# Second attention's scores on half arrays, two experts side by side

## The chip, the cores and the metric

The kernel runs on one core of a Trainium2 chip. The metric is the device time of one execution in microseconds; "before" is the median of three executions. A profile of one execution shows each engine's instructions in time: TensorE (PE for its matmuls, PEld for its weight loads), VectorE (DVE), ScalarE (ACT), GpSimd (POOL) and the DMA queue that SyncE (SP) issues to.

## The reference

The kernel computes three layers in a row: a windowed attention, a gated MLP, and a mixture of four attention experts. Only the last is touched by the change:

```python
def _moe2_ref(x, w_gate, wq, wk, wv, wo):          # x: 4 x 576 x 512, 4 experts, Hd = 64
    logits = x @ w_gate
    ...
    for e in range(E):
        q = x @ wq[e]; k = x @ wk[e]; v = x @ wv[e]
        scores = scale * (q @ k.transpose(0, 2, 1))
        scores = np.where(causal, -1000000000.0, scores)
        scores = scores - scores.max(-1, keepdims=True)
        a = np.exp(scores)
        a /= a.sum(-1, keepdims=True) + 1e-09
        ye = a @ v @ wo[e]
        ...                                         # weighted by the two best experts of a token
```

## The kernel before, in words

Precision comes from splitting: a float32 value is kept as a high part in the format float32r and a low part, the rounded difference. A product of two split values is three matmuls (high x high, high x low, low x high) accumulated in one PSUM bank.

**Order of the work.** Every piece of work is a node of a planner (class `Planner`, function `N`) with its engine or engines, a cost, the tiles it takes and the tiles it uses. The program is made of two plans that run one after the other (first attention and MLP, then the experts). In each, the planner walks through time and gives each engine the ready node of the lowest priority number; the table `SHIFT` moves units of work, `SWITCH` is added for a matmul node of another `form` (another division of TensorE's array) than the last, and `DRAIN` is what the planner books for such a change. The result is a fixed order on each engine.

**Banks.** PSUM has eight banks of 128 x 512 float32; they form one ring, `bank`, from which projections, scores, transposes and P V products all take.

**The experts.** Four batches (`b`), two pairs of experts (`pr`), two experts in a pair (`e` or `x`). The pair's q and k have 128 rows: expert 0 in rows 0 to 63, expert 1 in rows 64 to 127 (`HALF`).

- `c_qk` projects q or k of a pair for one half of the 576 tokens (288 columns, 12 matmuls) and splits the result. Each expert gets its own tiles: `qs[x]` holds the high part of q in the expert's own half and its low part in the other half; `kd[x]` holds the high part of k twice, in both halves (`twin` copies it over); `kz` (rings `r_kl`) holds the low part of k in the own half and zeros in the other (`zeros` fills them once). All these copies and subtractions work on 64 rows at a time.
- `unit` does one tile of 128 query rows of one expert: scores, mask and maximum, exponential with its sum, reciprocal, scaling of P by the sum and by the expert's weight, transpose of P, copy of it to `pg`. Query tile `I` = 0 to 3 sees 128 x (I + 1) keys. The scores (`s_mm`) are two matmuls over all 128 rows: (high, low) q against (high, high) k in `kd`, and the same q against (low, zero) k in `kz`, which together are the three products. The fifth tile (`last`) holds the last 64 queries of both experts, in two column halves of 288; there each half is four matmuls, two of them with 64 columns of weights, into one bank.
- `c_pv` multiplies P by v, two experts in the two column halves of the array; `c_wo` applies the output projection and stores.

Of the kernel before, what the change touches and what calls it, by code (L numbers as in the profile page):

```python
# [26 lines left out]
SWITCH = 107920.0  # L27
A_BIAS = 10098.0
C_BIAS = 162315.0
DVE_BIAS = (1136.0, 1147.0)  # L30
POOL_BIAS = (1131.0, 1068.0)
# [3 lines left out]
EFT = (636.0, 778.0)  # L35
# [54 lines left out]
class Node:  # L90
    __slots__ = ("on", "emit", "prio", "wait", "next", "ready", "alloc", "use", "end", "by", "late", "form", "nth", "sbuf")


class Planner:

    LAT = 200.0, 165.0, 130.0, 75.0, 900.0
    ISSUE, WAY, RATE, FLIGHT = 475.0, 650.0, 360.0, 8  # L100

    DRAIN = (0.0, 145.0, 145.0), (0.0, -78.0, 0.0), (0.0, 0.0, -78.0)

    CLASH, BEHIND = 1.0, 2200.0
# [164 lines left out]
def attn_gmlp_moe_kernel(ctx: ExitStack, tc: tile.TileContext, kq0, qT, kT, v, w_in, wspT, b_sp, w_outT,  # L269
# [30 lines left out]
    r_y = [Ring(lambda i=i: keep.tile([128, 2, S], F32, tag=f"y{i}", name=f"y{i}", bufs=1), 1, True) for i in range(6)]  # L300
# [875 lines left out]
    def unit(b, pr, e, I):  # L1176
# [3 lines left out]
        if last and e:  # L1180
            return
# [246 lines left out]
```

## Time and profile before

| | |
|---|---|
| time, median of 3 runs | 448.05 us (447.97, 448.05, 448.39) |
| span of the profiled execution | 447.1 us, mean granted clock of TensorE 1.000 |
| the profiled execution's own time | not recorded apart from the three runs; 448.05 - 447.1 = 0.95 us is taken for what lies around the span |
| TensorE busy | 438.9 us, 98% of the span, 3962 matmuls |
| TensorE weight loads busy | 396.0 us, 89% |
| VectorE, ScalarE, GpSimd busy | 310.9, 293.1, 107.4 us |

Busy times of TensorE contain overlaps: a matmul's row lasts from its start to its last result, and the next one starts before that. What one costs is read from one start to the next. The profile's groups name tiles, `bank<-kd,qs` being a matmul that writes `bank` and reads `kd` and `qs`; 128*64 is the part of the array it uses, rows by columns.

### The profile page before, as it was taken

What the parts mean: (1) busy time and instruction counts of PE and PEld (TensorE: products, weight loads), DVE (VectorE), ACT (ScalarE), POOL (GpSimd) and SP (SyncE); (2) the same over time, 40 slices, a digit from 0 to 9 for tenths busy, and PEclk for the clock granted to TensorE, in tenths of its full rate; (3) what the DMA queues carried; (4) which work ended last, traced back from release to release, by engine and by line L of the source; (5) the groups of instructions that cost most, each with busy time, mean ns of one, the idle gap of its engine ahead of it and who ended that gap; (6) DMA issues with size and microseconds to landing.
All of it is one profiled execution on the core that took longest, in us unless ns stands there. A gap on an engine that the chain in (4) does not pass through costs nothing.

```text
span 447.1 us, 10829 instructions
## 1 busy us (share of the span) xinstructions
PE 438.9 (98%) x3962; PEld 396.0 (89%) x3962; DVE 310.9 (70%) x1241; ACT 293.1 (66%) x926; POOL 107.4 (24%) x154
## 2 busy tenths in 40 slices
PE   8999999999999999999999999999999999999996
PEld 7977899989899879998899999789899978897875
DVE  4989989962875988024544556998697987787650
ACT  4989989662676969203322346987675978777863
POOL 4335782400310126000200251610031011011110
PEclk9999999999999999999999999999999999999999
DMA  7994837140242605003001000000010001000114
GB/s 280 281 330 122 251 101 221 45 140 0 64 138 64 179 7 144 0 1 95 1 1 48 0 1 1 1 2 1 1 48 25 1 2 48 0 2 25 71 53 160
DMA packets 31079, 33.10 MB, mean 74 GB/s; under 512 B 1905, under 2 KB 24689, under 8 KB 31026
## 3 DMA queue, kind: packets, MB, share of 16 engines
q1 hardware_dynamic: 31026, 32.41, 23.4%
q8 instruction: 31, 0.51, 0.5%
q14 instruction: 22, 0.18, 0.1%
HBM read 27.68 MB, written 4.72 MB: 72 GB/s over the span
## 4 chain that ended last, share of the span: by engine, by line
PE 87%; DVE 6%; ACT 4%; issue 2%; POOL 1%; POOLq 0%; ACTq 0%; DVEq 0%
PE bank L333 79%; PE bank L1238 5%; PE bank L564 3%; DVE p L1207 1%; ACT pa L552 1%; DVE qs L357 1%; POOL p L1222 1%; DVE p L1222 1%; ACT p L1218 1%; DVE pa L546 0%; ACT pa L558 0%; DVE pa L560 0%; DVE kz L357 0%; ACT pg L344 0%; ACT kd L344 0%
## 5 line engine op out<-in xcount | busy, mean ns | idle before, releaser
L333 PE MATMUL bank<-xh,w 128*128 128x288 f32 x512 | 109.6, 298 | 0.0
L333 PEld LDWEIGHTS bank<-xh,w 128*128 128x128 f32 x512 | 84.1, 188 | 0.9 <-DVE st L767 0.2
L333 PE MATMUL bank<-xl,w 128*128 128x288 f32 x256 | 75.3, 294 | 0.0
L333 PE MATMUL bank<-w,xh 128*128 128x512 f32 (+1 forms) x256 | 64.7, 342 | 0.2 <-ACT pt L344 0.2
L552 ACT ACTIVATE pa<-pa,mx 128x128 f32<-128x128 f32 x144 | 55.9, 400 | 5.4 <-DVE mx L546 5.4
L333 PEld LDWEIGHTS bank<-xl,w 128*128 128x128 f32 x256 | 48.2, 188 | 0.4
L333 PEld LDWEIGHTS bank<-w,xh 128*128 128x128 f32 x256 | 43.2, 188 | 5.7 <-ACT pt L344 0.5
L1218 ACT ACTIVATE p<-p,mc 128x128 f32<-128x128 f32 (+4 forms) x72 | 41.8, 582 | 8.4 <-DVE mc L1207 7.7
L1222 POOL TENSOR_SCALAR p<-p,mc,fx 128x256 f32<-128x256 f32 (+4 forms) x26 | 17.1, 658 | 111.3 <-DVE mc L1221 52.2
L333 PE MATMUL bank<-w,xl 128*128 128x512 f32 (+1 forms) x128 | 43.2, 338 | 0.0
L333 PE MATMUL bank<-wsp_h,vh 128*128 128x288 f32 x128 | 38.6, 302 | 0.0
L333 PE MATMUL bank<-wsp_h,vl 128*128 128x288 f32 x128 | 37.7, 295 | 0.0
L333 PE MATMUL bank<-wsp_l,vh 128*128 128x288 f32 x128 | 37.7, 294 | 0.0
L1207 DVE CUSTOM_DVE_ANT_0 p<-bank,cmask 128x128 f32<-128x128 f32 (+4 forms) x72 | 33.2, 482 | 5.2 <-PE bank L333 4.2
L770 POOL TENSOR_TENSOR st<-st,nhalf 128x1 f32<-128x1 f32 (+1 forms) x20 | 12.3, 615 | 98.7 <-DVE st L769 98.7
L344 ACT ACTIVATE pg<-bank 128x128 f32<-128x128 f32 (+4 forms) x71 | 29.1, 440 | 5.2 <-PE bank L1238 4.7
L546 DVE CUSTOM_DVE_ANT_0 pa<-bank,mask 128x128 f32<-128x128 f32 x120 | 28.4, 284 | 5.9 <-POOL mx L415 4.1
L1238 PE MATMUL bank<-ident,p 128*128 128x128 f32 x192 | 30.1, 278 | 1.5 <-POOL p L1222 0.7
L333 PE MATMUL bank<-kd,qs 128*128 128x128 f32 (+5 forms) x96 | 30.5, 335 | 0.0
L552 ACT ACTIVATION_READ_ACCUMULATOR pa<-pa,mx 128x1 f32 x144 | 28.6, 199 | 0.0
L333 PE MATMUL bank<-kz,qs 128*128 128x128 f32 (+5 forms) x96 | 28.4, 313 | 0.0
L835 DVE TENSOR_TENSOR y<-bank,ut 128x288 f32<-128x288 f32 x24 | 10.9, 454 | 24.9 <-PE bank L333 24.9
(209 smaller groups left out, 1083.4 us busy)
## 6 DMA issues: line engine op xcount, KB each, us to landing
vt<-in_v_dram SPq DMA_DIRECT2D x12, 512.0 KB, 4.9
qa<-in_qT_dram SPq DMA_DIRECT2D x44, 96.0 KB, 3.8
out_dram<-ot SPq DMA_DIRECT2D x15, 256.0 KB, 2.0
y<-in_w_in_dram SPq DMA_DIRECT2D x7, 512.0 KB, 7.3
kt<-in_kT_dram SPq DMA_DIRECT2D x12, 288.0 KB, 5.0
y<-in_w_outT_dram SPq DMA_DIRECT2D x4, 512.0 KB, 4.5
y<-in_wspT_dram SPq DMA_DIRECT2D x2, 576.0 KB, 4.2
vt<-in_kq_dram SPq DMA_DIRECT2D x2, 384.0 KB, 4.4
```

The costliest lines, as they stand in the source:

```text
L333: pe.matmul(o, lhsT, rhs, start=start, stop=stop)
L344: act.activation(o, i, AF.Copy)
L357: engs[e].tensor_tensor(out=o, in0=a, in1=hi.bitcast(F32), op=ALU.subtract)
L546: dve.tensor_tensor_reduce(out=pa[:, j, :], in0=ps[:, j * 128:(j + 1) * 128], in1=mask(j), scale=-0.125, scalar=3.0e38, op0=ALU.add, op1=A ...
L552: act.activation(pa[:, j, :], pa[:, j, :], AF.Exp, bias=mx[:, j, 0:1], scale=-1.0, accum_out=mx[:, j, 1:2])
L564: pe.transpose(ps2[:, j * 128:(j + 1) * 128], pa[:, j, :], ident)
L770: a = N((POOL, 464), lambda e: pool.tensor_tensor(out=st[:m, 9:10], in0=st[:m, 8:9], in1=nhalf[:m], op=ALU.pow), [n1], use=[st])
L835: dve.tensor_tensor(out=o, in0=ps[:, :HS], in1=u[:, d, tk], op=ALU.mult)
L1207: dve.tensor_tensor_reduce(out=P[:, a0:a1], in0=ps[:, :w], in1=msk, scale=-0.125, scalar=3.0e38, op0=ALU.add, op1=ALU.min, accum_out=mc[:, ...
L1218: a = N((ACT, 284 + 0.87 * L), lambda e: act.activation(P[:m, :L], P[:m, :L], AF.Exp, bias=mc[:m, 0:1], scale=-1.0, accum_out=mc[:m, 2:3]) ...
L1222: a = N({POOL: 328 + 0.832 * L, DVE: 90 + 0.52 * L}, lambda e: engs[e].tensor_scalar(P[:, :L], P[:, :L], mc[:, 3:4], fx[:, I, ev:ev + 1], ...
L1238: pe.transpose(ps[:, j * m:(j + 1) * m], P[:, j * 128:(j + 1) * 128], ident)
```

## The change

q and k of a pair are kept as plain parts in one tile `qk` of 128 rows and 4 x 576 columns: q high, q low, k high, k low, each with expert 0 in the upper and expert 1 in the lower rows. A score is then three products over 64 rows, and the same product of the two experts is issued one behind the other, on the upper and on the lower half of the array's rows, into two banks. Tiles 0 and 1 share one node and the same two banks; the fifth tile takes two nodes, each with two banks. Masking of the fifth tile is done in two pieces of 64 rows. The twin copies and the zero fills of `kz` go. P tiles become a ring of five that are freed in any order (before: four, in order). A fourth `form` is told to the planner, and the constants of its order (`SWITCH`, `DVE_BIAS`, `POOL_BIAS`, `EFT`, and the later entries of `SHIFT`) are other ones.

```diff
-    DRAIN = (0.0, 145.0, 145.0), (0.0, -78.0, 0.0), (0.0, 0.0, -78.0)
+    DRAIN = (0.0, 145.0, 145.0, 145.0), (0.0, -78.0, 0.0, 0.0), (0.0, 0.0, -78.0, 0.0), (0.0, 0.0, 0.0, 0.0)
...
-SWITCH = 107920.0
+SWITCH = 137658.0
...
+    r_qk = ring(p2, "qk", [128, 4 * S], F32R, 3)
...
-    r_p = ring(p2, "p", [128, S], F32, 4)
+    r_p = Ring(None, 5, tiles=[p2.tile([128, S], F32, name=f"p{i}") for i in range(5)])
...
     def c_qk(b, pr, h, nm):
...
-            def hi(e):
-                for x in range(2):
-                    copy(e, kd[x][HALF[x], tk], ps[HALF[x], :HS])
...
-            def twin(e):
-                for x in range(2):
-                    copy(e, kd[x][HALF[1 - x], tk], kd[x][HALF[x], tk])
...
+        a = N(on_copy(HS), lambda e: copy(e, qk[:, hi], ps[:, :HS]), [a], use=[ps, qk])
+        a = N((DVE, t_tt(HS)), lambda e: sub(e, qk[:, lo], ps[:, :HS], qk[:, hi]), [a], use=[ps, qk])
...
+    def scores(b, pr, tiles, prio):
+        qk = QK[b, pr]
+        def three(outs, q, k0, k1):
+            for n, (x, y) in enumerate(((0, 0), (0, 1), (1, 0))):
+                for e in range(2):
+                    mm(outs[e], qk[HALF[e], x * S + q[e]:x * S + q[e] + 128],
+                       qk[HALF[e], (2 + y) * S + k0:(2 + y) * S + k1], n == 0, n == 2)
...
+        ps, pp = [r_sc.new(), r_sc.new()], [r_p.new(), r_p.new()]
...
+        a = N((PE, sum(3 * t_mm(128 * I + 128) for I in tiles)), go, deps, alloc=ps + pp, use=[qk], prio=prio, form=3)
...
     def unit(b, pr, e, I):
...
+        if (b, pr, I) not in SC:
+            scores(b, pr, [0, 1] if I < 2 else [I], prio)
...
-                for x, c0, c1 in [(1, 448, S), (0, 512, S)] if last else [(e, 128 * I, 128 * I + m)]:
-                    mm_all(ps[:c1 - c0, :a1 - a0], [(qs[x][:, c0:c1], k[x][:, a0:a1]) for k in (kd, kl)])
...
+                    for y in range(2):
+                        dve.tensor_tensor_reduce(out=P[HALF[y], a0:a1], in0=ps[y][HALF[y], :HS],
...
```

On TensorE, the first scores of the second half, batch 0, pair 0. Before:

```order
L333 MATMUL bank_69<-kd,qs 128x128
L333 MATMUL bank_69<-kz_3559,qs 128x128
L333 MATMUL bank_66<-kd,qs 128x256
L333 MATMUL bank_66<-kz_3559,qs 128x256
L333 MATMUL bank_71<-kd,qs 128x128
L333 MATMUL bank_71<-kz_3560,qs 128x128
L333 MATMUL bank_72<-kd,qs 128x256
L333 MATMUL bank_72<-kz_3560,qs 128x256
```

The same scores (tiles 0 and 1 of both experts) with the change:

```order
L333 MATMUL bank_68<-qk 128x128
L333 MATMUL bank_69<-qk 128x128
L333 MATMUL bank_68<-qk 128x128
L333 MATMUL bank_69<-qk 128x128
L333 MATMUL bank_68<-qk 128x128
L333 MATMUL bank_69<-qk 128x128
L333 MATMUL bank_68<-qk 128x256
L333 MATMUL bank_69<-qk 128x256
L333 MATMUL bank_68<-qk 128x256
L333 MATMUL bank_69<-qk 128x256
L333 MATMUL bank_68<-qk 128x256
L333 MATMUL bank_69<-qk 128x256
```

Eight matmuls into four banks, expert by expert, have become twelve into two banks, the experts alternating.

On TensorE, a little later, around the first P V product (64x256 and 64x128 on `pg`), before:

```order
L333 MATMUL bank_72<-kd,qs 128x288
L333 MATMUL bank_72<-kz_3560,qs 128x288
L333 MATMUL bank_72<-kd,qs 64x288
L333 MATMUL bank_72<-kz_3559,qs 64x288
L333 MATMUL bank_68<-pg_3882,v_3583 64x256 x2
L333 MATMUL bank_68<-pg_3882,v_3583 64x128 x2
L333 MATMUL bank_70<-w,xh 128x260 x2
```

and with the change:

```order
L333 MATMUL bank_66<-qk 128x384
L333 MATMUL bank_71<-qk 128x384
L333 MATMUL bank_69<-pg_3855,v_3629 64x256 x2
L333 MATMUL bank_69<-pg_3855,v_3629 64x128 x2
L333 MATMUL bank_72<-qk 128x288
L333 MATMUL bank_68<-qk 128x288
L333 MATMUL bank_72<-qk 128x288
L333 MATMUL bank_68<-qk 128x288
L333 MATMUL bank_72<-qk 128x288
L333 MATMUL bank_68<-qk 128x288
L333 MATMUL bank_73<-xh,w 128x288
```

The P V product stands between two groups of scores now. Over the whole order, scores stood in 42 groups and P V products in 13 before; now scores stand in 21 and P V products in 9, and 12 times one of them follows the other directly.

On ScalarE, the copies of the first projections, before:

```order
L344 ACTIVATE kd<-bank_73 64x288 x2
L344 ACTIVATE kd<-kd 64x288 x2
L344 ACTIVATE v_3583<-bank_70 128x256
L344 ACTIVATE v_3583<-bank_68 128x256
L344 ACTIVATE v_3583<-bank_69 128x256
L344 ACTIVATE kd<-bank_66 64x288 x2
L344 ACTIVATE kd<-kd 64x288 x2
```

and with the change:

```order
L344 ACTIVATE qk<-bank_73 128x288
L344 ACTIVATE v_3629<-bank_70 128x256
L344 ACTIVATE qk<-bank_68 128x288
L344 ACTIVATE v_3629<-bank_69 128x256
L344 ACTIVATE qk<-bank_66 128x288
L344 ACTIVATE v_3629<-bank_71 128x256
L344 ACTIVATE v_3629<-bank_72 128x256
```

Four 64-row copies for each half of k, two of them twins, have become one copy of 128 rows.

## Rows read from the trace of the kernel before

**Rows 1.** Cores: span, mean granted clock of TensorE.
```profile
core 0: 447.1 us, clock 1.000
```

**Rows 2.** Stretches of time: busy us of PE, PEld, DVE, ACT, POOL (instructions), clock, DMA.
```profile
280.00:300.00 20.00, 19.23 (x143) 16.65 (x143) 19.34 (x84) 17.59 (x54) 9.48 (x10) 1.00 0.01 2
...
400.00:420.00 20.00, 20.00 (x143) 16.91 (x142) 15.80 (x67) 16.24 (x45) 3.60 (x6) 1.00 0.07 27
```

**Rows 3.** Waits of PE, 260 to 448 us: total us, times, longest us.
```profile
PE bank L1238 <- POOL p L1222: 0.7, 3, 0.3
PE bank L1238 <- DVE mc L1220: 0.5, 1, 0.5
PE bank L1238 <- DVE p L1222: 0.2, 1, 0.2
```

**Rows 4.** Instructions on tile kd: its matmuls, ns min/median/max.
```profile
L333 PE MATMUL bank<-kd,qs x96: 220/331/487, 279.5 to 424.8; 128*128 128x128 f32 x16, 128*128 128x256 f32 x16, 128*128 128x384 f32 x16, 128*128 128x512 f32 x16
```

**Rows 5.** PE in order of time, three stretches with scores: start us, latency us.
```profile
339.73 0.34 PE L333 MATMUL bank<-kd,qs 128*128 128x384 f32 x1
...
340.07 0.40 PE L333 MATMUL bank<-kd,qs 128*128 128x512 f32 x1
...
340.53 0.22 PE L333 MATMUL bank<-kd,qs 128*128 128x128 f32 x1
...
415.88 0.28 PE L333 MATMUL bank<-kd,qs 128*128 128x256 f32 x1
...
416.36 0.30 PE L333 MATMUL bank<-kd,qs 128*128 128x288 f32 x1
...
417.42 0.63 PE L333 MATMUL bank<-w,oh 128*128 128x512 f32 x2
...
424.64 0.23 PE L333 MATMUL bank<-kd,qs 128*128 128x128 f32 x1
...
425.04 1.59 PE L333 MATMUL bank<-w,ot 128*128 128x512 f32 x6
```

**Rows 6.** PE in order of time, first attention: three transposes and what follows.
```profile
20.18 0.49 PE L564 MATMUL bank<-ident,pa 128*128 128x128 f32 x3
20.51 0.39 PE L333 MATMUL bank<-ident 128*128 128x128 f32 x2
```

**Rows 7.** PE in order of time around a score step of the first attention.
```profile
82.22 0.82 PE L564 MATMUL bank<-ident,pa 128*128 128x128 f32 x6
82.97 0.89 PE L333 MATMUL bank<-kt,qa 64*64 64x128 f32 x24
83.78 0.40 PE L333 MATMUL bank<-xh,w 128*128 128x288 f32 x1
...
84.15 0.43 PE L333 MATMUL bank<-xh,w 128*128 128x288 f32 x2
```

**Rows 8.** Groups of weight loads by form: busy us, mean ns.
```profile
L333 PEld LDWEIGHTS bank<-kd,qs 128*128 128x128 f32 x80 | 15.3, 192 | 0.7 <-ACT v L344 0.2 <-issue 0.2
...
L333 PEld LDWEIGHTS bank<-kt,qa 64*64 64x64 f32 x432 | 11.6, 132 | 2.1 <-issue 0.8 <-DVE mx L546 0.3 <-DVE mx L570 0.2
```

**Rows 9.** Groups of DVE and ACT from 262 us on, half-height pieces: mean ns.
```profile
L357 DVE TENSOR_TENSOR qs<-bank,qs 64x288 fp32r<-64x288 f32 x32 | 14.6, 455 | 4.5 <-ACT qs L344 2.9 <-PE bank L1238 1.0
...
L344 ACT ACTIVATE kd<-kd 64x288 fp32r<-64x288 f32 x32 | 14.1, 440 | 0.5
...
L344 ACT ACTIVATE qs<-bank 64x288 fp32r<-64x288 f32 x32 | 12.9, 404 | 6.6 <-PE bank L333 6.2
```

**Rows 10.** Instructions on y and ut: full-height pieces of 288 columns, ns min/median/max.
```profile
L835 DVE TENSOR_TENSOR y<-bank,ut x24: 429/457/458, 73.4 to 199.3; 128x288 f32<-128x288 f32 x24
...
L352 ACT ACTIVATE ut<-bank x29: 384/410/414, 56.1 to 229.4; 128x288 f32<-128x288 f32 x29
```

More of the change, by code (lines that the diff above doesn't have):

```diff
@@ L26 @@
 N_Q = 6
-SWITCH = 107920.0
+SWITCH = 137658.0
 A_BIAS = 10098.0
 C_BIAS = 162315.0
-DVE_BIAS = (1136.0, 1147.0)
-POOL_BIAS = (1131.0, 1068.0)
+DVE_BIAS = (1104.0, 1251.0)
+POOL_BIAS = (1122.0, 1447.0)
 WARM = 8
@@ L34 @@
 LOADS = (-130000, -120000, -43801, -5807, 14591, 18276, 34028)
-EFT = (636.0, 778.0)
+EFT = (622.0, 777.0)
 U_CUT = 6
@@ L286, in attn_gmlp_moe_kernel @@
     ctx.enter_context(tc.manual_schedule())
-    ordered = ("xh", "xl", "xt", "kt", "vt", "pt", "vr", "vh", "vl", "qs", "kd", "v2", "vt2", "zt0", "zt1", "pg0", "pg1", "oh", "ol", "ot0", "ot1")
+    ordered = ("xh", "xl", "xt", "kt", "vt", "pt", "vr", "vh", "vl", "qk", "v2", "vt2", "zt0", "zt1", "pg0", "pg1", "oh", "ol", "ot0", "ot1")
     def ring(pl, tag, shape, dt, bufs):
@@ L969, in attn_gmlp_moe_kernel @@
     p2 = ctx.enter_context(tc.tile_pool(name="p2", bufs=1, reuse_waits="tile"))
-    r_kd = ring(p2, "kd", [128, S], F32R, 4)
-    KZ = [p2.tile([128, S], F32R, name=f"kz{i}") for i in range(4)]
+    r_qk = ring(p2, "qk", [128, 4 * S], F32R, 3)
     PG1 = [p2.tile([128, 4, 2, 320], F32, name=f"pg1{i}") for i in range(2)]
@@ L982, in zeros @@
     def zeros(pr):
-        for e in range(2):
-            i = 2 * pr + e
-            zero(("k", pr, e), [KZ[i][HALF[1 - e]].bitcast(F32)], 590.0)
         zero(("p", pr), [PG1[pr][HALF[1 - x], 3, :, x * 64:(x + 1) * 64] for x in range(2)], 200.0)
-    r_qs = ring(p2, "qs", [128, S], F32R, 4)
-    r_kl = [fixed(KZ[x::2]) for x in range(2)]
     r_v2 = ring(p2, "v2", [128, 4, 256], F32, 2)
@@ L1017, in y_deps @@
         return [n for c in range(NP) for n in ZN[b, c]], [s for c in range(NP) for s in YS[b, c]]
-    QS, KD, KL, QK_N, QK_PE = {}, {}, {}, {}, {}
+    QK, QK_N, QK_PE = {}, {}, {}
     def c_qk(b, pr, h, nm):
@@ L1025, in c_qk @@
         zn, zs = y_deps(b)
-        first = QK_PE.setdefault((b, pr, nm), [])
+        first = QK_PE.setdefault((b, pr), [])
         new = []
-        if h == 0 and nm == "q":
-            QS[b, pr] = new = [r_qs.new(), r_qs.new()]
-        elif h == 0:
-            KD[b, pr] = [r_kd.new(), r_kd.new()]
-            KL[b, pr] = [r.new() for r in r_kl]
-            new = KD[b, pr] + KL[b, pr]
+        if not first:
+            QK[b, pr] = r_qk.new()
+            new = [QK[b, pr]]
+        qk = QK[b, pr]
+        c = ("q", "k").index(nm) * 2 * S + h * HS
+        hi, lo = slice(c, c + HS), slice(c + S, c + S + HS)
         a = N((PE, 12 * t_mm(HS)), lambda e: mm3(ps[:, :HS], [
@@ L1036, in c_qk @@
               zn + W2_N[nm] + first, alloc=[ps] + new, use=zs + [wh, wl])
-        QK_PE[b, pr, nm] = [a]
-        if nm == "q":
-            qs = QS[b, pr]
-            def hi(e):
-                for x in range(2):
-                    copy(e, qs[x][HALF[x], tk], ps[HALF[x], :HS])
-            def lo(e):
-                for x in range(2):
-                    sub(e, qs[x][HALF[1 - x], tk], ps[HALF[x], :HS], qs[x][HALF[x], tk])
-            a = N(halves(HS), hi, [a], use=[ps] + qs)
-            a = N((DVE, 2 * t_tt(HS) + 185), lo, [a], use=[ps] + qs)
-        else:
-            kd, kl = KD[b, pr], KL[b, pr]
-            def hi(e):
-                for x in range(2):
-                    copy(e, kd[x][HALF[x], tk], ps[HALF[x], :HS])
-            def lo(e):
-                for x in range(2):
-                    sub(e, kl[x][HALF[x], tk], ps[HALF[x], :HS], kd[x][HALF[x], tk])
-            def twin(e):
-                for x in range(2):
-                    copy(e, kd[x][HALF[1 - x], tk], kd[x][HALF[x], tk])
-            n1 = N(halves(HS), hi, [a], use=[ps] + kl + kd)
-            n2 = N((DVE, 2 * t_tt(HS) + 185), lo, [n1], use=[ps] + kl + kd)
-            n3 = N(halves(HS, False), twin, [n1], use=kd, sbuf=True)
-            a = N({DVE: 0.0}, lambda e: None, [n2, n3])
+        QK_PE[b, pr] = first or [a]
+        a = N(on_copy(HS), lambda e: copy(e, qk[:, hi], ps[:, :HS]), [a], use=[ps, qk])
+        a = N((DVE, t_tt(HS)), lambda e: sub(e, qk[:, lo], ps[:, :HS], qk[:, hi]), [a], use=[ps, qk])
         QK_N.setdefault((b, pr, nm), []).append(a)
@@ L1174, in attn_gmlp_moe_kernel, with go @@
     PG, PG_N, OT, O_N, OT2, O2_N = {}, {}, {}, {}, {}, {}
+    SC = {}
+    def scores(b, pr, tiles, prio):
+        qk = QK[b, pr]
+        def three(outs, q, k0, k1):
[3 more added lines that the diff above has]
+                       qk[HALF[e], (2 + y) * S + k0:(2 + y) * S + k1], n == 0, n == 2)
+        deps = QK_N[b, pr, "q"] + QK_N[b, pr, "k"]
+        if tiles == [4]:
+            P, mc = r_p.new(), r_mc.new()
+            SC[b, pr, 4] = [], [], [P], mc
+            for i in range(2):
+                ps = [r_sc.new(), r_sc.new()]
+                a = N((PE, 3 * t_mm(HS)), lambda _, ps=ps, i=i: three(
+                    [p[:, :HS] for p in ps], (S - 64, S - 128), i * HS, (i + 1) * HS),
+                      deps + SC[b, pr, 4][0], alloc=ps + ([] if i else [P, mc]), use=[qk], prio=prio, form=3)
+                SC[b, pr, 4][0].append(a)
+                SC[b, pr, 4][1].append(ps)
+            return
+        ps, pp = [r_sc.new(), r_sc.new()], [r_p.new(), r_p.new()]
+        def go(_):
+            c = 0
+            for I in tiles:
+                w = 128 * I + 128
+                three([p[:, c:c + w] for p in ps], (w - 128, w - 128), 0, w)
+                c += w
+        a = N((PE, sum(3 * t_mm(128 * I + 128) for I in tiles)), go, deps, alloc=ps + pp, use=[qk], prio=prio, form=3)
+        c = 0
+        for I in tiles:
+            SC[b, pr, I] = a, ps, pp, c
+            c += 128 * I + 128
     def unit(b, pr, e, I):
@@ L1184, in unit @@
         ev = 2 * pr + e
-        both = range(2) if last else [e]
-        qs, kd, kl = QS[b, pr], KD[b, pr], KL[b, pr]
-        parts = [(0, HS), (HS, S)] if last else [(0, L)]
-        P, mc = r_p.new(), r_mc.new()
         fx, _, fn = FX[b]
-        tops = []
-        for i, (a0, a1) in enumerate(parts):
-            ps = r_sc.new()
-            def s_mm(_, ps=ps, a0=a0, a1=a1):
-                for x, c0, c1 in [(1, 448, S), (0, 512, S)] if last else [(e, 128 * I, 128 * I + m)]:
-                    mm_all(ps[:c1 - c0, :a1 - a0], [(qs[x][:, c0:c1], k[x][:, a0:a1]) for k in (kd, kl)])
-            def s_top(_, ps=ps, a0=a0, a1=a1, i=i):
-                w = a1 - a0
-                if not last:
-                    msk = cmask[:, 512 - L:512]
-                else:
-                    msk = cmask[:, 0:w] if i == 0 else tmask
-                dve.tensor_tensor_reduce(out=P[:, a0:a1], in0=ps[:, :w], in1=msk, scale=-0.125, scalar=3.0e38,
-                                         op0=ALU.add, op1=ALU.min, accum_out=mc[:, i:i + 1])
-            zn = [n for x in both for n in Z_N["k", pr, x]]
-            a = N((PE, 50 + 2 * len(both) * t_mm(a1 - a0, m)), s_mm, QK_N[b, pr, "q"] + QK_N[b, pr, "k"] + zn, alloc=[ps],
-                  use=[x[y] for x in (qs, kd, kl) for y in both], prio=prio)
-            tops.append(N((DVE, t_tt(a1 - a0)), s_top, [a] + tops[:1], alloc=[P, mc] if i == 0 else [],
-                          use=[ps] + ([] if i == 0 else [P, mc]), prio=prio))
@@ L1215, in unit @@
-        if len(parts) == 2:
-            tops = [N((DVE, 70), lambda e: dve.tensor_reduce(out=mc[:m, 0:1], in_=mc[:m, 0:2], axis=AX.X, op=ALU.min), tops, use=[mc], prio=prio)]
-        a = N((ACT, 284 + 0.87 * L), lambda e: act.activation(P[:m, :L], P[:m, :L], AF.Exp, bias=mc[:m, 0:1], scale=-1.0,
-                                                              accum_out=mc[:m, 2:3]), tops, use=[P, mc], prio=prio)
-        a = N((DVE, 70), lambda e: dve.tensor_scalar(mc[:m, 3:4], mc[:m, 2:3], 1e-9, None, op0=ALU.add), [a], use=[mc], prio=prio)
@@ L1221, in unit, with s_top @@
-        a = N((DVE, 75), lambda e: dve.reciprocal(mc[:m, 3:4], mc[:m, 3:4]), [a], use=[mc], prio=prio)
+        sn, banks_, pp, c0 = SC[b, pr, I]
+        P, mc, c0 = (pp[0], c0, 0) if last else (pp[e], r_mc.new(), c0)
+        cs = slice(c0, c0 + L)
+        if last:
+            tops = []
+            for i, (n, ps) in enumerate(zip(sn, banks_)):
+                a0, a1 = i * HS, (i + 1) * HS
+                def s_top(_, ps=ps, a0=a0, a1=a1, i=i):
+                    for y in range(2):
+                        dve.tensor_tensor_reduce(out=P[HALF[y], a0:a1], in0=ps[y][HALF[y], :HS],
+                                                 in1=cmask[HALF[y], 0:HS] if i == 0 else tmask[HALF[y]], scale=-0.125,
+                                                 scalar=3.0e38, op0=ALU.add, op1=ALU.min, accum_out=mc[HALF[y], i:i + 1])
+                tops.append(N((DVE, 2 * t_tt(HS) + 60), s_top, [n] + tops, use=ps + [P, mc], prio=prio))
+        else:
+            ps = banks_[e]
+            tops = [N((DVE, t_tt(L)), lambda _, ps=ps: dve.tensor_tensor_reduce(
+                out=P[:, cs], in0=ps[:, cs], in1=cmask[:, 512 - L:512], scale=-0.125, scalar=3.0e38,
+                op0=ALU.add, op1=ALU.min, accum_out=mc[:, 0:1]), [sn], alloc=[mc], use=[ps, P], prio=prio)]
@@ new lines, in unit @@
+        if last:
+            tops = [N((DVE, 70), lambda e: dve.tensor_reduce(out=mc[:, 0:1], in_=mc[:, 0:2], axis=AX.X, op=ALU.min), tops, use=[mc], prio=prio)]
+        a = N((ACT, 284 + 0.87 * L), lambda e: act.activation(P[:, cs], P[:, cs], AF.Exp, bias=mc[:, 0:1], scale=-1.0,
+                                                              accum_out=mc[:, 2:3]), tops, use=[P, mc], prio=prio)
+        a = N((DVE, 70), lambda e: dve.tensor_scalar(mc[:, 3:4], mc[:, 2:3], 1e-9, None, op0=ALU.add), [a], use=[mc], prio=prio)
@@ L1222, in unit @@
+        a = N((DVE, 75), lambda e: dve.reciprocal(mc[:, 3:4], mc[:, 3:4]), [a], use=[mc], prio=prio)
         a = N({POOL: 328 + 0.832 * L, DVE: 90 + 0.52 * L}, lambda e: engs[e].tensor_scalar(
-            P[:, :L], P[:, :L], mc[:, 3:4], fx[:, I, ev:ev + 1], op0=ALU.mult, op1=ALU.mult), [a, fn],
+            P[:, cs], P[:, cs], mc[:, 3:4], fx[:, I, ev:ev + 1], op0=ALU.mult, op1=ALU.mult), [a, fn],
               use=[P, mc, fx], prio=prio, sbuf=True)
@@ L1237, in tr @@
             for j in range(nj):
-                pe.transpose(ps[:, j * m:(j + 1) * m], P[:, j * 128:(j + 1) * 128], ident)
+                pe.transpose(ps[:, j * m:(j + 1) * m], P[:, c0 + j * 128:c0 + (j + 1) * 128], ident)
         def tc_(e_):
```

6 rows, old and new, of the table SHIFT are left out of this document.

## Prediction

> **What bounds the kernel now.** I read the span and clock first, then busy time by stretches, then what TensorE waited for, then the scores' own instructions and their order in time. The profiled execution spans 447.1 us at full granted clock [rows 1]; the median of the three runs is 448.05 us, so 0.95 us lie around the span, and I carry that over unchanged. The clock stays where it is: the change takes no long pause into TensorE's stream.
>
> In the two stretches shown from the second attention TensorE is busy 19.23 and 20.00 of 20 us, VectorE 19.34 and 15.80, ScalarE 17.59 and 16.24 [rows 2]. A busy TensorE includes overlapping ends, so the second reading is what it waited for: from 260 us on only 1.4 us in all (0.7, 0.5 and 0.2), each time a transpose waiting for a normalised P [rows 3]. So the second half runs at TensorE's pace, and what TensorE issues is what the time is made of. VectorE is the next one behind it, close in the first stretch only.
>
> **Durations.** The length of one matmul row is its latency. What it costs is the distance from its start to the next start. In [rows 5]: four 256-column score matmuls start within 0.48 us, 0.12 each; eight 288-column ones within 1.06, 0.1325 each, whether their weights have 128 columns or 64; two of 384 columns within 0.34, 0.17 each; two of 512 within 0.46, 0.23 each; four of 128 within 0.40, 0.10 each. Short ones cannot go below what their weights cost: three 128-column transposes take 0.33 us, 0.11 each [rows 6].
>
> **What is removed on TensorE.** The 96 matmuls on kd [rows 4] have as many on kz: 192. For one batch and one pair of experts: two experts, two matmuls each, for 128, 256, 384 and 512 keys, 4 x (0.10 + 0.12 + 0.17 + 0.23) = 2.48 us; the last tile, eight of 288 columns, 1.06. Together 3.54, times 8 (4 batches, 2 pairs) = 28.3 us.
>
> **What is added on TensorE.** 288 half-array matmuls, which are 144 rounds of two: three rounds for each width, six of 288 columns. If the two halves run side by side, a round costs what one full matmul of that width costs, with 0.11 as floor: 3 x (0.11 + 0.12 + 0.17 + 0.23) + 6 x 0.1325 = 1.89 + 0.80 = 2.69; times 8 = 21.5 us. That is 6.8 us less.
>
> No row of before has two halves with 128 columns of weights each. The nearest are the first attention's scores on quarter arrays: 24 instructions of 64 rows by 64 columns start and end within 0.81 us [rows 7]. One after the other at 0.11 they would need 2.64, so they run four at a time, upper and lower rows among them. But these are fp32 and move 128 columns in 0.11, half the rate of the 256 columns in 0.12 that the halves must keep up. So the bounds for the rounds are 21.5 us (side by side) and 43.0 us (one after the other); I take 21.5, by the row that is nearest. The Trainium skill (TensorE: Matmul & The Clock Gate, section Measured speedup vs the span model) reports 3.07 times, not 4, for four row tiles of 512 columns. By that the rounds would cost 28.0 us, my estimate from that page, and the sum below would turn from a gain of 2.1 us into a loss of 4.4; no row of before shows which.
>
> **Changing the array's division.** This is the cost that the change adds. A visit of the first attention's scores shows it: from the first of six transposes at 82.22 to the second-next projection matmul at 84.15 are 1.93 us [rows 7]; the work in it is 6 x 0.11 + 6 rounds x 0.11 + 2 x 0.1325 = 1.59. The other 0.34 us went into one change to quarters and one back: 0.17 each. Before, only the 64-column P V products leave the full array in the second half, 13 visits with 26 changes. By the new order there are 21 visits of scores and 9 of P V, 12 times directly next to each other: 48 changes. 22 more at 0.17 = 3.7 us. On top, the first load of each score visit has nothing to hide behind, and it is 128 columns wide where the quarters load 64: 192 against 132 ns [rows 8], 0.06 x 21 = 1.3 us. Bounds: a change could cost as little as 0.09 (the part that shows ahead of the quarters: six transposes need 0.66, and the quarters start 0.75 after them) with the first load hidden, 2.0 us in all; or, if one change of halves also empties what the other half holds, 0.25 and the load, 6.8.
>
> **Other engines.** q and k are split in one full-height piece. A half-height subtraction takes 455 ns [rows 9] and a full-height one of the same width 457 [rows 10]: height is free. So VectorE loses 64 x 0.455 and gains 32 x 0.457, less 14.5 us; the last tile's masked pass is cut into halves, 16 more at the 0.455 of such a piece, plus 7.3: net 7 us less. ScalarE loses about 64 copies of 0.404 and 32 twins of 0.440 [rows 9] and gains 32 of 0.410 [rows 10]: 27 us less. None of it lies on the path, since TensorE hardly waits; the most it can return is the 1.4 us of waits [rows 3]. The four zero fills go from POOL, off the path. What could take something back: a score step now asks for two of the eight banks and two of the five P tiles at once, so six softmax chains start together where before they started one by one. Bounds for the waits: all 1.4 us gone, or 2 us more (four waits like the longest, 0.5); I take 0.3 less, since the chains get shorter on both engines. DMAs, output stores and the first attention keep their order but for a handful of operations that change engine.
>
> **Sum.** -6.8 + 3.7 + 1.3 - 0.3 = -2.1 us against the profiled span, and so against the median: **445.9 us**.
>
> **Rivals.**
> 1. *A change of division is cheap for halves.* They divide rows only, and the columns stay whole, so perhaps only the emptying ahead of a visit is paid: 22 x 0.10 and no first load. Against it: the visit of the quarters lost as much again on the way in and out [rows 7]. -6.8 + 2.0 - 0.3 = -5.1, 442.9 us. Chance 0.13.
> 2. *The gain goes into waits.* In the first batch little other work is there to cover the six chains that start together, and near the end of the last batch as well; there VectorE is at 19.34 of 20 us already [rows 2]. The waits on P [rows 3] grow by 2 us instead of falling: -6.8 + 3.7 + 1.3 + 2.0 = +0.2, 448.2 us. For it: bursts of scores that fill all eight banks. Against it: 7 us less on VectorE, 27 less on ScalarE. Chance 0.14.
> 3. *The halves hinder each other (slower).* If the weight loads of upper and lower rows go one after the other, a round takes at least 2 x 0.11 = 0.22: 3 x (3 x 0.22 + 0.23) + 6 x 0.22 = 3.99, times 8 = 31.9 us, 10.4 more than side by side; -2.1 + 10.4 = +8.3, 456 us. One after the other altogether would be +19. It decides from the point where a round costs a tenth more than one full matmul (2.1 of 21.5). Against it: the quarters' four loads and matmuls fit one round of 0.11. For it: nothing here runs two halves at the full rate. The skill's rule above is a milder form, 452 us. Chance 0.15, both forms together.
> 4. *Changes cost 0.25 and nothing else gives*: -6.8 + 6.8 = 0, 448 us. Chance 0.06.
>
> **How the numbers follow.** About 0.9 us (0.2%) is what a measurement can tell from no change. The forecast has 0.52 and a range of its own of 444.2 to 447.4; a tenth of it falls within 0.9 us of before. Faster: 0.47 + 0.13 + a little of the second rival = 0.63. Same: 0.05 + most of rivals 2 and 4 = 0.17. Slower: 0.15 and the bad ends of 2 and 4 = 0.20. The range that should hold 8 in 10 goes from the first rival's 442.9 up over rivals 2 and 4, with another 1.2 us of waits: 442.9 to 449.4; most of rival 3 stays outside.
>
> **What would show it.** Side by side: in the order in time the two matmuls of a round start within some 10 ns and rounds of 288 columns follow at 0.13, of 512 at 0.23; rival 3 shows 0.22 or more for 288. The changes: 0.17 lost ahead of and behind each visit, with a first round longer by the load. The waits of TensorE after 260 us stay near 1.4 us; several us there are rival 2. The half copies and twins are gone from ScalarE. I am wrong if the rounds are not at one matmul's pace, or if the stream of TensorE is shorter by 2 us and the time is not.

## The result and the profile after

The changed kernel takes 442.62 us (median of 4 runs, 442.44 to 444.11); the kernel before took 448.18 us beside it (4 runs, 447.97 to 448.39). The ratio is 0.9887, with a 95% interval of 0.9871 to 0.9903: 5.6 us faster. The forecast was 445.9 us, 2.1 us faster, with a range from 442.9: right in direction, but the gain came out more than twice as large and just outside the range.

The core's span and clock, for [rows 1]:

```profile
core 0: 440.5 us, clock 0.999
```

The same two stretches of the second half as in [rows 2] (busy us of PE, PEld, DVE, ACT, POOL, then clock and DMA):

```profile
280.00:300.00 20.00, 20.00 (x182) 18.37 (x182) 14.68 (x62) 14.04 (x41) 6.08 (x7) 1.00 0.00 1
400.00:420.00 20.00, 19.86 (x144) 15.09 (x145) 16.89 (x75) 15.47 (x43) 2.15 (x3) 1.00 0.14 53
```

In the first stretch TensorE is now busy throughout. It issues 182 matmuls instead of 143, but 58 of them are half-array scores, where 35 full-array ones stood before. Meanwhile VectorE falls from 19.34 to 14.68 us and ScalarE from 17.59 to 14.04. The view of the waits, which showed 1.4 us for TensorE before [rows 3], shows none from 255 us on.

The instructions on the new tile `qk` (ns min/median/max, first and last start), for [rows 4, 9, 10]:

```profile
L333 PE MATMUL bank<-qk x288: 217/294/499, 276.8 to 414.5; 64*128 64x288 f32 x48, 64*128 64x128 f32 x24, 64*128 64x256 f32 x24, 64*128 64x384 f32 x24
L344 ACT ACTIVATE qk<-bank x32: 390/410/414, 263.2 to 399.5; 128x288 fp32r<-128x288 f32 x32
L357 DVE TENSOR_TENSOR qk<-bank,qk x32: 437/458/460, 265.8 to 400.0; 128x288 fp32r<-128x288 f32 x32
```

A full-height copy takes 410 ns and a full-height subtraction 458, as the prediction took from half-height 404 and 455. So half of each is gone, and the 32 twins with them.

TensorE in order of time around the first visit of scores (start us, latency us):

```profile
276.42 0.30 PE L333 MATMUL bank<-xl,w 128*128 128x288 f32 x1
276.55 0.29 PE L333 MATMUL bank<-xh,w 128*128 128x288 f32 x1
276.77 1.48 PE L333 MATMUL bank<-qk 64*128 64x128 f32 x18
278.19 0.40 PE L333 MATMUL bank<-xh,w 128*128 128x288 f32 x1
278.43 0.29 PE L333 MATMUL bank<-xl,w 128*128 128x288 f32 x1
```

The row `x18` merges eighteen half-array matmuls (three rounds each of 128, 256 and 384 columns); they take 1.42 us from 276.77 to 278.19. From the trace's single starts, the two of a round begin 0 to 15 ns apart, mostly 3 or 4. Inside a visit a round takes, as the median, 0.112 us (128 columns), 0.120 (256), 0.133 (288), 0.174 (384) and 0.233 (512): a full matmul's pace in [rows 5]. The first round of each visit takes longer, by 0.05 us at 128 columns and 0.10 at the wider ones.

The share of the chain of work that ended last, by engine, from the page of the changed kernel:

```profile
PE 95%; DVE 4%; issue 0%; ACT 0%; POOL 0%; POOLq 0%; ACTq 0%; DVEq 0%
```

and from the page of the kernel before, run once more (the first experiment):

```profile
PE 88%; DVE 6%; ACT 2%; issue 1%; POOL 1%; POOLq 0%; ACTq 0%; DVEq 0%
```

Before, about an eighth of that chain ran over other engines. The prediction did not read this view.

**An account of the second half.** From the first projection of the experts to the start of the last matmul, before takes 181.95 us (181.99 in the repeat) and the changed kernel 176.61: 5.3 us less, nearly the whole gain. To split it, I went through TensorE's starts in the trace: wherever the next one came more than 0.11 us later than its width's pace allows, the excess over the pace counts as lost (P V products, whose starts are uneven, only when far off). This gives 3.1 us in before (3.2 in the repeat) and 0.4 after. The view of the waits shows 1.4 us in before. So by this count the gain is 2.7 us of lost time and 2.6 us of the stream itself. The split depends on the limit: at 0.25 us instead of 0.11, lost time is 2.5 us before and 0.3 after, 2.2 less, and the stream 3.2 less. Below, "lost" is the sum with 0.11.

### The profile page after: what moved, and what is told of

It is laid out like the page before. It is cut to its first block, busy times and chain, and to the rows that moved or that the text cites. A ratio compares the mean times of both kernels' runs of the same rounds, so it can differ in the third digit from the quotient of the medians.

```text
span 440.5 us, 10970 instructions
## 1 busy us (share of the span) xinstructions
PE 434.4 (99%) x4058; PEld 390.5 (89%) x4058; DVE 291.2 (66%) x1225; ACT 268.5 (61%) x871; POOL 105.7 (24%) x157
## 4 chain that ended last, share of the span: by engine, by line
PE 95%; DVE 4%; issue 0%; ACT 0%; POOL 0%; POOLq 0%; ACTq 0%; DVEq 0%
PE bank L333 86%; PE bank L1235 5%; PE bank L564 4%; DVE p L1202 1%; DVE p L1209 1%; DVE pa L546 1%; DVE p L1219 0%; DVE pa L560 0%; PE bank L1252 0%; DVE mc L1218 0%; DVE ot L348 0%; DVE bank L686 0%; DVE y L696 0%; DVE y L688 0%; ACT ot L344 0%
## 5 line engine op out<-in xcount | busy, mean ns | idle before, releaser
L1215 ACT ACTIVATE p<-p,mc 128x384 f32<-128x384 f32 (+4 forms) x72 | 41.5, 578 | 16.9 <-DVE mc L1209 14.7
L1219 POOL TENSOR_SCALAR p<-p,mc,fx 128x128 f32<-128x128 f32 (+4 forms) x33 | 20.4, 620 | 110.8 <-DVE mc L1218 64.5
L1209 DVE CUSTOM_DVE_ANT_0 p<-bank,cmask 128x384 f32<-128x384 f32 (+3 forms) x64 | 28.6, 486 | 8.6 <-PE bank L333 8.2
L344 ACT ACTIVATE pg<-bank 128x512 f32<-128x512 f32 (+4 forms) x79 | 30.1, 438 | 2.3 <-PE bank L1235 2.0
L552 ACT ACTIVATION_READ_ACCUMULATOR pa<-pa,mx 128x1 f32 x144 | 29.8, 207 | 0.0
L1235 PE MATMUL bank<-ident,p 128*128 128x128 f32 x192 | 27.4, 276 | 0.1
L333 PE MATMUL bank<-qk 64*128 64x288 f32 (+4 forms) x288 | 27.2, 325 | 0.0
L333 PEld LDWEIGHTS bank<-w,xl 128*128 128x128 f32 x128 | 24.1, 188 | 2.8
```

Of the source, the lines that this page charges most:

```text
L333: pe.matmul(o, lhsT, rhs, start=start, stop=stop)
L344: act.activation(o, i, AF.Copy)
L552: act.activation(pa[:, j, :], pa[:, j, :], AF.Exp, bias=mx[:, j, 0:1], scale=-1.0, accum_out=mx[:, j, 1:2])
L1209: tops = [N((DVE, t_tt(L)), lambda _, ps=ps: dve.tensor_tensor_reduce(out=P[:, cs], in0=ps[:, cs], in1=cmask[:, 512 - L:512], scale=-0.125 ...
L1215: a = N((ACT, 284 + 0.87 * L), lambda e: act.activation(P[:, cs], P[:, cs], AF.Exp, bias=mc[:, 0:1], scale=-1.0, accum_out=mc[:, 2:3]), to ...
L1219: a = N({POOL: 328 + 0.832 * L, DVE: 90 + 0.52 * L}, lambda e: engs[e].tensor_scalar(P[:, cs], P[:, cs], mc[:, 3:4], fx[:, I, ev:ev + 1], ...
```

## The experiments

**The kernel before once more.** No edit. The two first profiles already differ by 1.3 us where the second half starts (261.25 and 259.98 us), ahead of nearly everything the change touches.

> The kernel before, unchanged, profiled once more. In the two profiles the first half (up to the first projection of the experts) took 261.25 us before and 259.98 after, with the same TensorE order. Theory 'chance': the 1.3 us are a matter of the execution, and this profile starts its second half anywhere from 259.9 to 261.3, most likely near 260.0. Theory 'constants': it starts at 261.2 again. The second half should take 182.0 us to the last matmul in both.

447.79 us, span 446.0; its second half starts at 260.08 us and takes 181.99. The 1.3 us in the first half is chance; the 5.3 in the second is not. TensorE's longest wait in this run, in order of time:

```profile
288.23 0.22 PE L333 MATMUL bank<-kd,qs 128*128 128x128 f32 x1
288.29 0.27 PE L333 MATMUL bank<-kz,qs 128*128 128x128 f32 x1
289.09 0.55 PE L1238 MATMUL bank<-ident,p 128*128 128x128 f32 x3 [0.53 <-DVE mc L1220]
```

The bracket says 0.53 us of idle time; from start to start it is 0.80 where a matmul of 128 columns costs 0.11, so 0.69 is lost. The view counts idle time from a matmul's modelled end, which lies 0.27 us behind its start, and so misses what overlaps with that latency. What the transposes waited for, from the chain of waits of this run (start us, us, what):

```profile
286.77 0.37 DVE p L1207
287.14 0.01 DVE mc L1207
287.15 0.07 DVE mc L1220
287.21 0.33 DVE ol L357
287.55 0.07 DVE mc L1221
287.62 0.05 DVE mc L1216
287.67 1.36 DVE p L1222
289.03 0.07 DVE mc L1220
289.10 0.53 PE bank L1238 x3
```

The chain runs on VectorE: maxima, reciprocals, a split and the scaling of P follow one another without a gap.

**Relief alone.** The kernel before with its full-array scores and its order, but q and k copied and split in one piece of 128 rows, and no twins:

```diff
-                for x in range(2):
-                    copy(e, qs[x][HALF[x], tk], ps[HALF[x], :HS])
+                copy(e, qs[0][:, tk], ps[:, :HS])
...
-                for x in range(2):
-                    sub(e, kl[x][HALF[x], tk], ps[HALF[x], :HS], kd[x][HALF[x], tk])
+                sub(e, kl[0][:, tk], ps[:, :HS], kd[0][:, tk])
...
-                for x in range(2):
-                    copy(e, kd[x][HALF[1 - x], tk], kd[x][HALF[x], tk])
+                pass
```

> The kernel before, its scores on the full array, in its own order on every engine, but q and k split in one piece of 128 rows each and without twin copies: the experts' own layout is left out, so both experts' scores are computed from the same tiles and the output is another one. ScalarE does about 27 us less and VectorE 15 us less; TensorE's matmuls are as before. Theory 'relief pays by itself': TensorE's 3.6 us of waits in the second half (182.0 us) fall to about 0.5 and the time to about 445.3 us. Theory 'relief pays only with the new order' (the new order was made for short splits, the old one for long ones): less than 1 us, 447.3 or more.

445.56 us, ratio 0.9951 (0.9938 to 0.9965): 2.2 us gained with not one matmul removed. The two experts' own layout is left out here, so the output is another one; the number and the shapes of TensorE's matmuls are those of before. Its stretches:

```profile
280.00:300.00 20.00, 19.88 (x157) 17.49 (x158) 17.73 (x83) 14.70 (x46) 9.29 (x10) 1.00 0.00 1
400.00:420.00 20.00, 20.00 (x143) 16.69 (x142) 13.36 (x57) 13.54 (x37) 3.18 (x5) 1.00 0.13 49
```

TensorE is busy 19.88 us of the first stretch, against 19.23 before [rows 2], and issues 157 matmuls in it instead of 143. Lost time falls from 3.1 to 1.4 us. The prediction had put this very part off the path and allowed 0.3 us for it.

**The changed kernel without the one-piece split.** Copies and subtractions of q and k in two 64-row pieces; scores, order and the missing twins stay:

```diff
-        a = N(on_copy(HS), lambda e: copy(e, qk[:, hi], ps[:, :HS]), [a], use=[ps, qk])
-        a = N((DVE, t_tt(HS)), lambda e: sub(e, qk[:, lo], ps[:, :HS], qk[:, hi]), [a], use=[ps, qk])
+        a = N(on_copy(HS), lambda e: [copy(e, qk[HALF[x], hi], ps[HALF[x], :HS]) for x in range(2)], [a], use=[ps, qk])
+        a = N((DVE, t_tt(HS)), lambda e: [sub(e, qk[HALF[x], lo], ps[HALF[x], :HS], qk[HALF[x], hi]) for x in range(2)], [a], use=[ps, qk])
```

> The changed kernel with the copies and subtractions of q and k issued in two pieces of 64 rows again, in the same order on every engine: ScalarE and VectorE get 32 x 0.41 = 13 and 32 x 0.46 = 15 us of work back, TensorE's order is the same. Theory 'relief' (TensorE's waits went because these engines have less to do): 1.5 to 2.7 us of waits come back, about 444.5 us. Theory 'order' (they went because the new order asks for nothing too early): less than 0.7 us, at most 443.3.

447.20 us, ratio to before 0.9981 (0.9969 to 0.9994): 4.6 us of the 5.6 are gone, more than expected. TensorE's waits after 262 us (total, times, longest):

```profile
PE bank L333 <- ACT pg L344: 1.0, 3, 0.5
PE bank L1235 <- POOL p L1219: 1.0, 3, 0.5
PE bank L1235 <- DVE p L1219: 0.3, 1, 0.3
```

**Which of the two.** Once the copies alone in two pieces (first line of the edit), once the subtractions alone (second line).

> The changed kernel with only the copies of the high parts in two pieces of 64 rows (13 us more on ScalarE), the subtractions in one. Both splits in pieces cost 4.6 us. Theory 'ScalarE': 3 us or more of it, 445.6 or more. Theory 'VectorE': 1.5 us or less, at most 444.1. Theory 'the length of the chain from projection to scores counts, not the engine': about half, 444.9.

> The changed kernel with only the subtractions of the low parts in two pieces of 64 rows (15 us more on VectorE), the copies in one. Theory 'VectorE': 3 us or more of the 4.6, 445.6 or more. Theory 'ScalarE': 1.5 us or less, at most 444.1. Theory 'the chain from projection to scores': about half, 444.9.

445.20 us (ratio 0.9937, 0.9917 to 0.9957) with the copies in pieces and 446.25 (0.9964, 0.9952 to 0.9976) with the subtractions: 2.6 and 3.6 us more than the changed kernel, 6.2 together against 4.6 for both at once. The subtractions come out as theory 'VectorE' said, the copies between the theories. Both engines' pieces stand in the chains that TensorE waits for, VectorE's the heavier, and they partly cover each other.

**The twins as well.** The kernel with copies and subtractions in two pieces and, behind each copy of k, two more 64-row copies on ScalarE:

```diff
+    tw = p2.tile([128, 272], F32R, name="tw")
...
+        a = N(on_copy(HS), lambda e: [copy(e, qk[HALF[x], hi], ps[HALF[x], :HS]) for x in range(2)] + [
+            copy(e, tw[HALF[1 - x], :], qk[HALF[x], hi][:, :272]) for x in range(2) if nm == "k"], [a], use=[ps, qk])
```

> The changed kernel with the copies and subtractions of q and k in two 64-row pieces and, behind each copy of k, two more 64-row copies on ScalarE (272 columns, into a tile that nothing reads) as the twins were: 32 of about 0.43 us, 14 us of ScalarE. The order of the nodes stays. This leaves of the change only the scores on half arrays and the new order. Theory 'relief is on the path': the split pieces alone gave 447.2; the twins stand between the copies and the softmax work on ScalarE and add 1 to 3 us: 448 to 450, so without the relief the half arrays give nothing over the kernel before (448.2). Rival 'the gains add up': relief alone gave 2.4 us of the 5.6 in the order of before, so without it 442.6 + 2.4 to 2.6 = 445.1. Rival 'twins beside the path': 447.2, as with the pieces alone.

452.71 us, ratio 1.0111 (1.0096 to 1.0126). Half arrays and the new order without the relief are 4.9 us *slower* than before (447.86 beside it), more than the theory expected. The waits and the place of the longest one:

```profile
PE bank L333 <- ACT pg L344: 2.0, 4, 1.1
PE bank L1237 <- POOL p L1221: 0.8, 3, 0.4
PE bank L1237 <- DVE p L1221: 0.4, 2, 0.2
```

```profile
283.49 0.50 PE L333 MATMUL bank<-qk 64*128 64x512 f32 x1
285.09 0.96 PE L333 MATMUL bank<-qk 64*128 64x512 f32 x5 [1.11 <-ACT pg L344]
```

One matmul of the first round starts, and the next stands for 1.6 us until ScalarE has copied the transposed P out of a bank (`pg`), late because it was copying twins. That is the second rival's mechanism, a score step that asks for two banks at once; here it is real, in the changed kernel it does not arise. Behind this wait the clock falls, as the windows of 4 us show:

```profile
284.00:288.00 4.00, 2.91 (x19) 2.23 (x19) 3.68 (x10) 3.94 (x11) 0.97 (x1) 0.79 0.01 2
288.00:292.00 4.00, 4.00 (x30) 2.82 (x27) 3.27 (x13) 2.75 (x8) 1.46 (x3) 0.79 0.02 4
```

The granted clock is 0.79 over these 8 us, so part of them ran at the lower level (1.2 GHz): 8 x 0.21 = 1.7 us more, an estimate. The rest of the 10.1 us to the changed kernel is mostly in shorter waits.

**The order of before.** The changed kernel with `SWITCH`, the biases, `EFT` and `SHIFT` of before:

```diff
-SWITCH = 137658.0
+SWITCH = 107920.0
...
```

> The changed kernel with all of the order's constants of before (SWITCH, DVE_BIAS, POOL_BIAS, EFT, SHIFT). Theory 'order': TensorE's waits in the second half come back, 2 to 4 us, and more visits of the halves at 0.4 each: 446 us or more. Theory 'relief': waits stay under 1 us, and only the added visits count: 442.5 to 444.5.

458.18 us, ratio 1.0207 (1.0179 to 1.0235), 15.6 us slower than with its own order. Two waits, 7.0 us together, are the largest part:

```profile
PE bank L1235 <- DVE p L1219: 5.0, 1, 5.0
PE bank L1235 <- POOL p L1219: 2.0, 1, 2.0
```

and behind the first one the clock (three stretches of the second half):

```profile
262.00:320.00 58.00, 57.49 (x477) 52.04 (x477) 40.13 (x194) 32.00 (x99) 16.91 (x23) 1.00 0.01 2
320.00:336.00 16.00, 11.01 (x70) 8.58 (x68) 11.82 (x36) 8.55 (x22) 2.79 (x2) 0.79 0.00 0
336.00:456.00 120.00, 114.60 (x867) 93.78 (x865) 68.61 (x313) 67.15 (x196) 15.52 (x21) 0.98 0.12 41
```

TensorE stood idle until 326.5 us; the granted clock had fallen just before, and from 326 to 332 us it was 0.50, the lower of the two levels (1.2 GHz). So the new constants belong to the change. What they do alone, for the kernel before, was not tried, nor was the ring of five P tiles taken out by itself.

**The first plan's constants.** The entries for the first half are other ones too. Here those of before, everything else as changed:

```diff
-DVE_BIAS = (1104.0, 1251.0)
-POOL_BIAS = (1122.0, 1447.0)
+DVE_BIAS = (1136.0, 1251.0)
+POOL_BIAS = (1131.0, 1447.0)
...
-EFT = (622.0, 777.0)
+EFT = (636.0, 777.0)
```

> The changed kernel with the first plan's constants of before (entries 0 of DVE_BIAS, POOL_BIAS and EFT, SWITCH in the first plan, one entry of SHIFT), the second plan as changed. Theory 'constants': 1.3 us slower than the changed kernel, 443.9. Theory 'chance': the same within 0.4 us, 442.6.

442.87 us, ratio 0.9872 (0.9852 to 0.9892), second half 176.74: no difference.

**The experts in turn.** Three products of one expert on the upper rows, then three of the other on the lower, instead of alternating:

```diff
-            for n, (x, y) in enumerate(((0, 0), (0, 1), (1, 0))):
-                for e in range(2):
+            for e in range(2):
+                for n, (x, y) in enumerate(((0, 0), (0, 1), (1, 0))):
```

> The changed kernel with the three products of one expert issued before the three of the other, in place of the two experts alternating. Theory 'side by side, issued in order': only the third product of one and the first of the other overlap, five rounds for three, 2/3 of the 20 us of rounds more: about 13 us more, 456. Theory 'the halves run freely': no change, 442.6. Theory 'they never overlapped': no change either, but then the alternating rounds would show 0.26 us for 288 columns, and the trace of the changed kernel shows 0.13.

443.17 us in a single run, second half 176.68 against 176.61. The first visit:

```profile
277.41 1.49 PE L333 MATMUL bank<-qk 64*128 64x128 f32 x18
278.83 0.40 PE L333 MATMUL bank<-xh,w 128*128 128x288 f32 x1
```

1.42 us for the 18, the same as when they alternate. The first starts within the visit, ns, from the trace:

```
alternating:  0   4   166  170   275  278   390  394   559  562
in turn:      0  10   165  175   274  284   389  399   558  568
```

They start in pairs in both kernels; issued in turn, the second of a pair comes mostly 10 ns behind the first instead of 3 to 4. The trace names the rows' number and not which half, so that each half takes its own products in turn is the reading that fits, not a thing the rows say.

**The price of a change of the array's division.** The changed kernel with one full-array matmul (256 columns, overwritten at once) between tile 0 and tile 1 in the 8 visits that hold both: 16 more changes.

```diff
+                if I == 1:
+                    mm(ps[0][:, c:c + w], qk[:, :128], qk[:, 2 * S:2 * S + w])
                 three([p[:, c:c + w] for p in ps], (w - 128, w - 128), 0, w)
```

> The changed kernel with one full-array matmul (256 columns, result overwritten at once) between the products of tile 0 and those of tile 1 in each of the 8 visits that hold both: 8 matmuls at 0.12 us and 16 more changes of the array's division, nothing else. Theory 'a change costs 0.17 to 0.20' (0.40 a visit measured): 8 x (0.12 + 0.40) = 4.2 us more, 446.8; in order of time the first round of tile 1 starts 0.6 us behind the last of tile 0 instead of 0.12. Rival 'only the emptying ahead is paid, 0.10 a visit': 8 x 0.22 = 1.8, 444.4. Rival '0.25 a change and the load': 8 x (0.12 + 0.56) = 5.4, 448.0. If waits elsewhere absorb part of it the total is less than the sum of the gaps.

446.23 us, ratio 0.9965 (0.9956 to 0.9975): 3.6 us more. The first visit:

```profile
277.29 0.29 PE L333 MATMUL bank<-xh,w 128*128 128x288 f32 x1
277.52 1.95 PE L333 MATMUL bank<-qk 64*128 64x128 f32 x19
279.39 0.40 PE L333 MATMUL bank<-xh,w 128*128 128x288 f32 x1
```

From 277.52 to 279.39 are 1.87 us, where the changed kernel takes 1.42: 0.45 more, 0.12 of it the matmul itself. So two changes cost 0.33, 0.17 each, and 8 x 0.45 = 3.6 us is the whole difference. The first load behind each change is in that price.

**The account over all of it.** The time is the median of the runs; the other columns are from the one profiled execution.

| kernel | time, us | second half | lost | second half less lost |
|---|---|---|---|---|
| before, repeat | 447.8 | 182.0 | 3.2 | 178.8 |
| relief alone, scores and order of before | 445.6 | 179.8 | 1.4 | 178.4 |
| the change | 442.6 | 176.6 | 0.4 | 176.2 |
| experts in turn | 443.2 | 176.7 | 0.4 | 176.3 |
| copies in pieces | 445.2 | 178.8 | 2.4 | 176.4 |
| subtractions in pieces | 446.2 | 180.2 | 3.6 | 176.6 |
| both in pieces | 447.2 | 181.4 | 4.6 | 176.8 |
| first plan's constants of before | 442.9 | 176.7 | 0.4 | 176.3 |
| both, and twins | 452.7 | 186.8 | 8.6 | 178.2 |
| order of before | 458.2 | 192.5 | 12.5 | 180.0 |

Apart from the last two rows, the last column has two levels: 178.4 to 178.8 with full-array scores in the old order, 176.2 to 176.8 with half arrays in the new one. The stream gives some 2.3 us; the rest is how long TensorE stands. The last two rows hold stretches at the lower clock, whose longer matmuls are in part counted as lost and in part left in the last column; they were not taken apart further. The relief is worth 2.2 us to the kernel before and 10.1 us (452.7 - 442.6) to the changed one, whose order was made with the relief in it and was not made anew without it.

## Why the prediction was wrong

- **The rounds: right.** Side by side at one matmul's pace, 21.7 us for the 144 rounds by the paces above, where 21.5 were forecast. The third rival (a round at least 0.22) falls: 288 columns follow at 0.133. (The 0.81 us in which the prediction lets the 24 quarter-array instructions start and end is the distance from their first start to the next matmul's start; their row lasts 0.89 [rows 7].) The Trainium skill (TensorE: Matmul & The Clock Gate, section Measured speedup vs the span model) gives 3.07 times for four row tiles, by which the rounds would have cost 28.0 us, an estimate from that page; with two halves the runs show no such loss.
- **The changes of division: right.** 0.17 was taken from a visit of quarter arrays, and the added changes show 0.17 for halves. The rivals of 0.10 and of 0.25 (a figure for which the prediction has no row) fall. That the first rival's 442.9 us lies next to the measured 442.62 is luck: its cheap changes are not what the runs show. The separate 1.3 us for the first loads was charged too much, at least in part: the measured price holds a load, and a whole visit (276.55 to 278.43, 1.88 us, less 1.22 for the rounds and 0.27 for two full matmuls) shows 0.39, or 0.20 a change with everything in it. The Trainium skill (TensorEngine Tiling (Array Packing), section Key Properties) says that changing the mode drains the engine; the runs agree that a change costs time, 0.17 us.
- **The stream as a whole: forecast 1.8 us less, measured about 2.6.** The rounds at 21.7 us for the removed 28.3 and 22 changes at 0.17 to 0.20 with the load in them make 2.2 to 2.9 less. The missing 0.8 us fit the first loads, which were charged beside changes that already hold a load.
- **The waits: wrong, and this is the step that failed.** "None of it lies on the path, since TensorE hardly waits; the most it can return is the 1.4 us of waits [rows 3]", and 0.3 of that was taken. By the count above they returned 2.7 us (2.2 at the wider limit): 2.4 of the 3.2 us by which the second half beat the sum. Two errors lie in it. The view's 1.4 us were taken as all that TensorE loses, where its starts show 3.1. And 0.3 was taken from it, although the relief stood right in the chains that ended those waits: the kernel with the relief alone gains 2.2 us, and the changed one, in its own order, loses 4.6 with the pieces halved again and 10.1 with the twins as well. The chain of work that ended last had 6% on VectorE and 2 to 4% on ScalarE, and VectorE's 19.34 of 20 us [rows 2] stood in the prediction's own text, as a fact about the second place instead of as a bound of that stretch: with the relief alone TensorE issues 157 of the same matmuls in it instead of 143.
- **Other engines: sizes partly right.** ScalarE is busy 268.5 us instead of 293.1: 24.6 less, where 27 were forecast. VectorE has 291.2 instead of 310.9: 19.7 less, where 7 were forecast, since the new order also gives 8 of VectorE's copies of P to ScalarE and 7 scalings of P to GpSimd (33 instead of 26), and the scalings that stay take less time (last section).
- **The second rival: its mechanism exists, its condition does not.** Two banks asked for at once stop TensorE for 1.11 us when the twins are back, and for nothing in the changed kernel. The rival and the relief belonged together, as I read it: the bursts of scores cost what the other engines cannot take away in time.
- **The clock: right for the change** (0.999). In the two variants with the longest waits it fell and cost extra.
- **The base.** 0.95 us was set around the span by pairing a span with the median of other runs. With both from one execution it is 447.79 - 446.0 = 1.8 us before and 442.44 - 440.5 = 1.9 after; this does not touch the difference.

## What to carry to other kernels

Where TensorE is busy for nearly the whole span, count its lost time from start to start and read the chain that ended last beside the waits: here the waits showed 1.4 of 3.1 us, and an eighth of the chain lay elsewhere. Work taken from VectorE and ScalarE is worth what stands behind it in the chain to the next matmul, and that worth differs with the scores and the order: 2.2 us with full-array scores in the old order, 10.1 with half arrays in the new one. How much of this is the denser bursts of scores and how much the order is not shown. A change of division between the full and the half array cost 0.17 us here, and a whole visit 0.39, so half arrays pay where a visit saves more than that.

## What the runs showed of the hardware that was not expected

- The order of issue did not matter to the pace: 18 half-array products take 1.42 us whether the halves alternate or three products of one half are issued ahead of three of the other.
- A long wait of TensorE is paid twice. After the 5.0 us wait of the kernel in the old order, the granted clock was 0.79 over 320 to 336 us (16 x 0.21 = 3.4 us less at full clock, some 0.3 of it still within the wait); after the 1.1 us wait and its neighbours in the kernel with twins, 0.79 over 284 to 292.
- One scaling of P by VectorE (128 x 384) took 1.36 us at 287.67 us in the repeat of before, in the chain to the longest wait, where the line's median in the first profile is 0.48. GpSimd was subtracting 128 x 576 tiles at that time (287.39 to 290.31). No experiment tried whether that is the cause, but the traces fit it:

```profile
287.39 2.92 POOL L357 TENSOR_TENSOR xl<-y,xh 128x576 fp32r<-128x576 f32 x2
287.65 1.38 DVE L1222 TENSOR_SCALAR p<-p,mc,fx 128x384 f32<-128x384 f32 x1
```

  In the traces of all runs, every scaling of P on VectorE beside which GpSimd stood idle took its width's median within 5%, and each longer one overlapped work of GpSimd. The overlapped ones took 3.8 us more than their widths' medians in before, 3.4 with the relief alone, 3.5 in the changed kernel with the old order and 0.7 with the new one. So some 3 us of VectorE's relief came with the order, not with the one-piece split.
